# Chunk-selected attention and a gated MLP on one core: halved maxima for four pairs, not three, an order held as ranks, and the first tile's bounds left out

## The chip, the cores and the metric

The kernel runs on one core of a Trainium2 chip. A core has five engines that run their own instruction queues in order: TensorE (PE; its weight loads are listed as PEld), VectorE (DVE), ScalarE (ACT), GpSimd (POOL) and SyncE (SP, which here only issues DMAs). They wait for each other by semaphores. The metric is the device time of one execution in microseconds (us); a kernel's time is the median of its runs.

## The reference

Inputs are q, k and v of shape (4 batches, 8 heads, 768 tokens, 64), and the weights of a gated MLP. Attention reads only 6 chosen chunks of 32 keys per query; its output feeds the MLP:

```python
k_min, k_max = np.min(k_chunks, axis=3), np.max(k_chunks, axis=3)      # 24 chunks of 32 keys
ub = np.sum(np.maximum(q * k_min, q * k_max), axis=-1)                 # bound of a chunk's scores
ub = np.where(causal, ub, -1000000000.0)
top_chunks = np.argsort(ub, axis=-1)[..., -6:]
scores = scale * np.matmul(q, k.transpose(0, 1, 3, 2))
scores = np.where(sel & (pos[:, None] >= pos[None, :]), scores, -1000000000.0)
attn = np.exp(scores - np.max(scores, axis=-1, keepdims=True))
attn = attn / (np.sum(attn, axis=-1, keepdims=True) + 1e-09)
x = np.matmul(attn, v)                                                 # heads side by side: (4, 768, 512)
h = np.maximum(x @ w_in, 0.0); u, v = h[..., :512], h[..., 512:]
v_n = (v - mean(v)) / np.sqrt(var(v) + 1e-06)
out = (u * (np.einsum('ts,bsd->btd', w_spatial, v_n) + b_spatial[None, :, None])) @ w_out
```

## The kernel before

The work is cut into 16 *pairs* p of heads (4 per batch; the two heads lie on partitions 0 to 63 and 64 to 127) and into one gated MLP per batch b. Tokens go by 6 tiles i of 128. All of it is a list of 1,395 *pieces* (`work_list`, L251), each with a name, an engine or two that can do it, the pieces that it comes after, and the buffers that it fills and reads. For a pair they are, in this order:

- `load`, `cast` (L626, L635): k, q and v by DMA, mostly from SP, then as 16-bit numbers; `turn`/`kT`/`qT` bring k and q to head dimension by token, on TensorE with a copy on ScalarE or, for pairs 5 to 15, by a transposing DMA; `qp` (L679) is max(-q, 0).
- `ext` (L666, VectorE): maximum and negated minimum of each chunk of keys. `bounds` (L692, TensorE): the bound of each chunk for each query by three products per tile and head; for pairs below `EARLY` = 6 a product of `big` and `far` ahead of them pushes the future chunks down, for later pairs `ub` (L704) adds a constant. `top` and `leave` (L713, L720, VectorE): the sixth largest bound of tiles 1 to 5 and the chunks under it; tile 0 has but four chunks and none is left out.
- `pk` (L770, TensorE) and `mx` (L792, VectorE): all scores once, and each chunk's largest. For pairs below `FOLD` = 3 the part off the diagonal goes another way: `kd` (L738, GpSimd) is the difference of a chunk's two halves, `fd` (L742, TensorE) its product with q, `fr` (L751, ScalarE) the positive part, `fi` and `fb` (L755, L760, TensorE) add that to the scores of the second half, so that VectorE reads half as many numbers. The diagonal blocks (`end_product`, L730) are made alike for all.
- `minus`, `kept`, `shift`: the largest score over the chosen chunks (the shift of the exponential); `turn_bias` (L826, TensorE) and `bT` bring bias and shift to the other side, with six products of 64 rows, two at a time.
- `probs` (L843, TensorE): scores by key and query, with the bias added by a second product; `ex` (L867, ScalarE): the exponentials, in five strips of 512 columns and one of 128 for both heads; `cut` (L874, GpSimd): the causal part of the diagonal blocks; `weigh` (L880, TensorE): the product with v and a column of ones; `av`, `sum`, `inv`, `norm`: division by the sum, on GpSimd or VectorE; `xT`: transposed, mostly by a DMA from SP.

For a batch: `hv`, `vr`, `bn`, `rstd0` to `2`, `vn` (the normalised half), `hu`, `uT` (the other half), `mix`, `ms`, `plus`, `gT` (the spatial product, bias and gate), `og`, `oe`, `od` (the output). TensorE's PSUM has three buffers "two" for scores and exponents and two "mg" for the rest; in the last batch the MLP uses both.

What sets the order: `Work.order` (L114) runs a small planner, with a cost in us written beside each piece (`took` by engine) and a rank for each from the table `RANK`; each engine takes the ready piece of lowest rank whose buffers are free by the planner's clock. `WHERE` names the engine of each piece that has a choice. The result is one list, and each engine's instructions are issued in its order. Products of 64 rows (`TILED`, L100) and of 128 alternate in TensorE's queue.

Of the kernel before, what the change touches and what calls it, by code (L numbers as in the profile page):

```python
# [16 lines left out]
P = 128  # L17
# [66 lines left out]
"""  # L84
WHERE = """
AAAAGAGAGVGVGAAVAGAGAGVVAGAGAGAVVVVVAVAVAAAAAVVAVGGGGVGGAAVAAAAAAAAAAAVVAVAVVAAVAAVVGGGGGVVAAAAA
# [3 lines left out]
class Work:  # L90
# [8 lines left out]
    DELAY = {"PE": 0.25, "DVE": 0.17, "ACT": 0.18, "POOL": 0.14, "SP": 0.0}  # L99
    TILED = ("pk", "probs", "bounds", "turn_bias", "fd", "fb")  # L100
# [12 lines left out]

    def order(self):  # L114

        pieces, n = self.pieces, len(self.pieces)
        users, slot, freed_at, done_at = {}, {}, {}, {}
        slots = {tag: [None] * k for tag, k in self.bufs.items()}
        then, todo, ready_at, begun = [[] for _ in range(n)], [0] * n, [0.0] * n, [False] * n
        for i, (_, _, _, after, new, old, _) in enumerate(pieces):  # L120
            for b in new + old:
                users[b] = users.get(b, 0) + 1
            for a in after:
                then[self.index[a]].append(i)
                todo[i] += 1
        rank, where = [int(x) for x in RANK.split()], iter(WHERE.replace("\n", ""))
        engine = dict(P="PE", V="DVE", A="ACT", G="POOL", S="SP")
        assert len(rank) == n
        for i, (name, on, _, after, new, old, dma) in enumerate(pieces):
            if len(on) > 1:  # L130
                e = engine[next(where)]
                on = {e: on[e]}
# [934 lines left out]
```

## Time and profile before

| | |
|---|---|
| median of 3 runs | 249.05 us (248.89 to 249.26) |
| the profiled execution | 248.22 us, its span 246.5 us |
| PE busy | 224.9 us, 91% |
| DVE busy | 206.5 us, 84% |
| ACT busy | 191.9 us, 78% |
| POOL busy | 165.9 us, 67% |
| granted TensorE clock | 1.00 |

The span runs from the first instruction of an engine to the end of the last store. A line of a view by stage gives the busy time of each engine in a stretch; a line of the groups gives a source line, engine, operation, what it writes and reads, how often, its busy time and mean length, and the idle time before it with what ended it; a line of the chain gives a start, a length and what the end waited for.

### The profile page before, as it was taken

How to read it: one execution, taken by the hardware profiler on the slowest of the kernel's cores; microseconds unless marked ns; L12 is line 12 of the kernel's file. 1: busy time of each engine (PE TensorE's matmuls, PEld its weight loads, DVE VectorE, ACT ScalarE, POOL GpSimd, SP SyncE). 2: the span in 40 equal slices, each digit the busy share in tenths (PEclk: the TensorE clock that was granted, in tenths of full speed). 3: DMA queues.
4: the chain of work that ended last, by engine and by line, in shares of the span. 5: the costliest groups of instructions: out<-in, count | busy, mean ns of one | idle time of the engine just before them, and what ended most of it. 6: DMA issues, size and time to landing. Idle time of an engine off the chain costs nothing.

```text
span 246.5 us, 9019 instructions
## 1 busy us (share of the span) xinstructions
PE 224.9 (91%) x3780; PEld 144.6 (59%) x3780; DVE 206.5 (84%) x512; ACT 191.9 (78%) x298; POOL 165.9 (67%) x209
## 2 busy tenths in 40 slices
PE   0898778878999999999999999999999999999993
PEld 0656457666755675666665576666745566645551
DVE  4799999999999999799998997899998853349670
ACT  3598887979998999587859897897679969767312
POOL 8879749887785377999965929999926147402160
PEclk9999999999999999999999999999999999999999
DMA  7969996699999949484899997128900010350005
GB/s 189 325 186 201 257 242 127 122 164 241 168 186 235 216 82 187 89 170 112 190 161 271 175 200 125 34 75 140 268 22 19 0 36 0 105 188 0 0 28 227
DMA packets 93895, 35.51 MB, mean 144 GB/s; under 512 B 86208, under 2 KB 90144, under 8 KB 93856
## 3 DMA queue, kind: packets, MB, share of 16 engines
q1 hardware_dynamic: 91568, 31.81, 61.9%
q0 software_dynamic: 2016, 2.75, 6.5%
q8 instruction: 29, 0.48, 0.8%
q10 hardware_dynamic: 272, 0.39, 0.5%
q14 instruction: 10, 0.08, 0.1%
HBM read 24.77 MB, written 6.29 MB: 126 GB/s over the span
## 4 chain that ended last, share of the span: by engine, by line
PE 48%; DVE 28%; ACT 14%; DMA 4%; issue 3%; POOL 2%; DVEq 0%; ACTq 0%
DVE cmax L807 11%; PE mg L1001 11%; ACT pr L871 8%; PE mg L1024 6%; PE mg L885 5%; PE two L856 4%; PE mg L937 3%; PE two L863 3%; DVE stats L954 3%; DVE ext L671 3%; PE two L786 3%; DVE top L715 2%; PE mg L990 2%; DMA k<-in_k_dram 2%; DVE cmax L801 2%
## 5 line engine op out<-in xcount | busy, mean ns | idle before, releaser
L871 ACT ACTIVATE pr<-two 128x1024 f16<-128x1024 f32 (+1 forms) x96 | 85.3, 934 | 5.4 <-PE two L863 4.8
L807 DVE TENSOR_REDUCE cmax<-two 128x24 f32<-128x768 f32 (+4 forms) x104 | 85.3, 843 | 3.5 <-PE two L735 2.0
L856 PE MATMUL two<-qT,kT 64*128 64x128 f16 (+3 forms) x384 | 40.5, 258 | 5.4 <-ACT bT L835 1.9
L863 PE MATMUL two<-bT,member 64*128 64x128 f16 (+1 forms) x512 | 39.7, 233 | 0.0
L877 POOL TENSOR_SCALAR_AFFINE_SELECT pr<-pr 128x768 f16<-128x768 f16 x32 | 27.9, 886 | 9.1 <-ACT pr L871 9.0
L1019 POOL TENSOR_TENSOR vr<-tmp,uT 128x384 f16<-128x384 f32 x27 | 24.5, 922 | 11.9 <-DVE tmp L1012 11.8
L671 DVE TENSOR_REDUCE ext<-kT 128x24 f16<-128x768 f16 x32 | 29.5, 936 | 1.9 <-ACT kT L617 1.7
L1001 PE MATMUL mg<-wsT,vn 128*128 128x384 f16 x168 | 30.2, 327 | 0.0
L856 PEld LDWEIGHTS <-kT 64*128 64x128 f16 x384 | 19.9, 94 | 17.2 <-issue 15.1
L863 PEld LDWEIGHTS <-member 64*128 64x128 f16 x512 | 25.7, 94 | 5.1
L885 PE MATMUL mg<-v,pr 128*128 128x65 f16 x672 | 25.9, 194 | 0.7 <-POOL pr L877 0.5
L786 PE MATMUL two<-kT,qT 64*128 64x384 f16 (+4 forms) x182 | 24.6, 280 | 1.4 <-ACT pr L871 0.5
L885 PEld LDWEIGHTS <-pr 128*128 128x128 f16 x672 | 23.1, 98 | 3.6 <-issue 1.0
L1001 PEld LDWEIGHTS <-vn 128*128 128x128 f16 x192 | 17.7, 98 | 12.2 <-issue 0.6
L990 PE MATMUL mg<-xT,w_in_sb 128*128 128x384 f16 x112 | 22.4, 328 | 0.0
L907 POOL TENSOR_TENSOR x<-av,rc 128x768 f16<-128x768 f32 x11 | 16.2, 1469 | 8.8 <-DVE rc L900 4.9
L732 PE MATMUL two<-kT,qT 64*128 64x128 f16 x192 | 19.6, 221 | 2.3 <-ACT qT L617 1.0
L1024 PE MATMUL mg<-w_out_sb,vr 128*128 128x512 f16 x84 | 20.8, 380 | 0.0
L937 PE MATMUL mg<-w_in_sb,xT 128*128 128x512 f16 x84 | 20.3, 380 | 0.4 <-DVE o L619 0.4
L889 ACT COPY av<-mg 128x390 f32<-128x390 f32 x32 | 15.6, 500 | 6.2 <-PE mg L885 6.0
L954 DVE BATCH_NORM_STATS2 stats<-vr 128x6 f32<-128x512 f32 x24 | 16.6, 692 | 4.0 <-ACT vr L942 2.9
L735 PE MATMUL two<-half_ahead,ident 64*128 64x64 f16 x192 | 19.8, 193 | 0.0
(113 smaller groups left out, 496.8 us busy)
## 6 DMA issues: line engine op xcount, KB each, us to landing
q<-in_q_dram SPq DMA_DIRECT2D x16, 384.0 KB, 6.4
v<-in_v_dram SPq DMA_DIRECT2D x16, 384.0 KB, 5.7
out_dram<-o SPq DMA_DIRECT2D x24, 256.0 KB, 2.1
k<-in_k_dram SPq DMA_DIRECT2D x15, 384.0 KB, 5.7
vr<-in_moe_w_spatial_dram POOLq DMA_DIRECT2D x6, 192.0 KB, 5.6
w_in_sb<-in_moe_w_in_dram POOLq DMA_DIRECT2D x4, 256.0 KB, 8.8
w_out_sb<-in_moe_w_out_dram POOLq DMA_DIRECT2D x4, 128.0 KB, 4.5
k<-in_k_dram ACTq DMA_DIRECT2D x1, 384.0 KB, 4.7
```

Source lines behind the costliest of these rows:

```text
L671: nc.vector.tensor_reduce(held["ext", p][:, m], src, axis=AX.X, op=Alu.min if m else Alu.max, negate=(m == 1))
L786: mm(t[:, h, o:o + before], lhsT=qT[rows[h], c], rhs=kT[rows[h], a * CH:a * CH + before], start=True, stop=True)
L807: nc.vector.tensor_reduce(tops(p)[:, i // 2, :, i % 2, a:z], held["two", (p, u)][:, :, o:o + n].rearrange("p h (c e) -> p h c e", e=CH), a ...
L856: mm(t[:, h, z:z + n * P], lhsT=kT[rows[h], keys], rhs=qT[rows[h], i * P:(i + n) * P], start=True, stop=False)
L863: mm(d, lhsT=member[rows[h], r, keys], rhs=bT[rows[h], m * P:(m + w_) * P].rearrange("c (m s) -> c m s", s=P), start=False, stop=(n == 1 o ...
L871: nc.scalar.activation(out=held["pr", p][:, :, c0:c0 + n], in_=held["two", (p, "e", c0)][:, :, 0:n], func=Act.Exp, scale=scale)
L877: nc.gpsimd.affine_select(out=d, in_=d, compare_op=Alu.is_ge, fill=0.0, base=0, channel_multiplier=-1, pattern=[[0, NT], [1, P]])
L885: mm(a[:, i, :], lhsT=pr[:, at[t, i]:at[t, i] + P], rhs=vp[:, h * NT + t, :], start=(t == 0), stop=(t == i))
L937: mm(t, lhsT=held["xT", b][:, ko, i * P:(i + 1) * P], rhs=w_in_sb[:, ko, DH:2 * DH], start=(ko == 0), stop=(ko == NDO - 1))
L990: mm(t, lhsT=w_in_sb[:, ko, db * P:(db + 1) * P], rhs=held["xT", b][:, ko, s * HS:(s + 1) * HS], start=(ko == 0), stop=(ko == NDO - 1))
L1001: mm(t, lhsT=held["vn", b][:, si, db * P:(db + 1) * P], rhs=wsT[:, si, s * HS:(s + 1) * HS], start=(si == 0), stop=(si == NT - 1))
L1024: mm(t, lhsT=held["vr", ("g", b)][:, ko, i * P:(i + 1) * P], rhs=w_out_sb[:, ko, :], start=(ko == 0), stop=(ko == KO - 1))
```

## The change

1. `FOLD` is 4: pair 3's maxima are halved as those of pairs 0 to 2.
2. `bounds` leaves out the three products of tile 0; what remains for tile 0 is the product of `big` and `far`, for all pairs.
3. A `turn_bias` with neighbours of 128 rows on both sides in TensorE's queue is made with products of 128 rows (the other head's rows meet zeros of the identity), one at a time. In the new order these are pairs 5, 6 and 9.
4. `RANK` is a new table and is now the order itself, a permutation of the 1,398 pieces; the planner with its clock is gone, and a buffer goes to the slot whose last user stands earliest. `WHERE` is new too: `norm` is on GpSimd for 14 pairs (before 11), `gT` on VectorE for 10 pieces (before 5), and some single pieces change engines, among them `qp` of pair 0 (from ScalarE to VectorE).
5. Some costs in the list are other numbers; with the planner gone nothing reads them.

```diff
 RANK = """
-0 9 100 7 13 10 5 1 28 103 118 168 128 124 256 303 296 313 298 327 425 450 446 421 430 435 398 407 417 422 403 411 388
+1 12 207 2 21 5 4 3 81 366 138 175 174 164 200 276 322 321 287 320 570 565 564 413 435 440 419 421 402 409 383 394 393
...
 WHERE = """
-AAAAGAGAGVGVGAAVAGAGAGVVAGAGAGAVVVVVAVAVAAAAAVVAVGGGVGGAAVAAAAAAAAAAAVVAVAVVAAVAAVVGGGGGVVAAAAA
+AAVAGVGAGAGVGAAVAGAGAGAVVGAGAGVGAGAGAAAVAAAAAVVVVGVVVGVVAAAAAAAVAAAAVVVVVAAAAVAAVAGGVVGGVVAAAAVA
...
+    EITHER = ("turn_bias",)
...
+        for (name, on, _, _, _, _, _), at in zip(pieces, rank):
+            result[at] = name, engine[next(where)] if len(on) > 1 else next(iter(on)), at
+        done = set()
+        for at, (name, _, _) in enumerate(result):
+            _, _, _, after, new, old, _ = pieces[self.index[name]]
+            for b in new:
+                tenants = held[b[0]]
+                free = [(-1 if x is None else last[x], k) for k, x in enumerate(tenants) if x is None or users[x] == 0]
+                slot[b] = min(free)[1]
+                tenants[slot[b]] = b
...
-FOLD = 3
+FOLD = 4
...
+    turned = [name for name, e, _ in order if e == "PE"]
+    whole = {name[1] for a, name, z in zip(turned, turned[1:], turned[2:])
+             if name[0] in Work.EITHER and not (a[0] in Work.TILED or z[0] in Work.TILED)}
...
-            each = [(big, far[:, i])] * (p < EARLY) + [(qT[:, c], x[:, 0]), (qp[:, c], x[:, 0]), (qp[:, c], x[:, 1])]
+            each = [(big, far[:, i])] * (p < EARLY or i == 0) + [(qT[:, c], x[:, 0]), (qp[:, c], x[:, 0]), (qp[:, c], x[:, 1])] * (i > 0)
...
-                r = slice(g * D, (g + 1) * D)
-                mm(t[:, g, m * D:(m + 1) * D], lhsT=bias[slot["bias", p]][r, 4 * m:4 * m + 4, :].rearrange("p g c -> p (g c)"), rhs=ident[r, r], start=True, stop=True)
+                r, c = slice(g * D, (g + 1) * D), slice(0, P)
+                if p in whole:
+                    r, c = c, r
+                mm(t[:, g, m * D:(m + 1) * D], lhsT=bias[slot["bias", p]][r, 4 * m:4 * m + 4, :].rearrange("p g c -> p (g c)"),
+                   rhs=ident[r, c] if p in whole else ident[r, r], start=True, stop=True)
```

More of the change, by code (lines that the diff above doesn't have):

```diff
@@ L1 @@
-import heapq
 import math
@@ L116, in order @@
         pieces, n = self.pieces, len(self.pieces)
[L117 to L120, printed above, removed]
+        rank, where = [int(x) for x in RANK.split()], iter(WHERE.replace("\n", ""))
+        engine = dict(P="PE", V="DVE", A="ACT", G="POOL", S="SP")
+        assert sorted(rank) == list(range(n))
@@ L121, in order @@
+        users, slot, last, result = {}, {}, {}, [None] * n
+        held = {tag: [None] * k for tag, k in self.bufs.items()}
+        for _, _, _, _, new, old, _ in pieces:
             for b in new + old:
                 users[b] = users.get(b, 0) + 1
[L123 to L132, printed above, removed]
-            pieces[i] = (name, on, rank[i], after, new, old, dma)
-        free = {e: 0.0 for e in self.ENGINES}
-        ready = {e: [] for e in self.ENGINES}
-        events = [(0.0, i) for i in range(n) if todo[i] == 0]
-        t, bus, late, tiled, result = 0.0, 0.0, 0.0, False, []
-        def place(i):
-            got = []
-            if any(b not in slot for b in pieces[i][5]):
-                return None
-            for tag, key in pieces[i][4]:
-                for k, b in enumerate(slots[tag]):
-                    if b is None or freed_at.get(b, t + 1) <= t + 1e-9:
-                        got.append(((tag, key), k))
-                        break
-                else:
-                    return None
-            return got
@@ L153, in begin @@
-        def begin(e):
-            nonlocal bus, late, tiled
-            aside, found = [], False
-            while ready[e] and not found:
-                due, i = heapq.heappop(ready[e])
-                if begun[i]:
-                    continue
-                got = place(i)
-                if got is None:
-                    aside.append((due, i))
-                    continue
-                found = begun[i] = True
-                name, on, _, _, new, old, dma = pieces[i]
-                result.append((name, e, t))
-                took = on[e]
-                if e == "PE" and tiled != (name[0] in self.TILED):
-                    tiled, took = not tiled, took + 0.095
-                free[e] = t + took
-                if dma:
-                    if e == "POOL":
-                        late = max(late, t + took + 0.2)
-                        both = max(0.0, bus - late)
-                        bus += min(both, dma)
-                        late += 4 * dma if dma <= 0.25 * both else 0.75 * both + dma
-                        done = late + 0.8
-                    else:
-                        bus = max(bus, t + took + 0.4)
-                        both = max(0.0, late - bus)
-                        bus += 4 * dma if dma <= 0.25 * both else 0.75 * both + dma
-                        done = bus + 0.8
-                else:
-                    done = t + took + self.DELAY[e]
-                for b, k in got:
-                    slot[b] = k
-                    slots[b[0]][k] = b
-                for b in new + old:
-                    done_at[b] = max(done_at.get(b, 0.0), done)
-                    users[b] -= 1
-                    if users[b] == 0:
-                        freed_at[b] = done_at[b]
-                        heapq.heappush(events, (freed_at[b], -1))
-                for j in then[i]:
-                    todo[j] -= 1
-                    ready_at[j] = max(ready_at[j], done)
-                    if todo[j] == 0:
-                        heapq.heappush(events, (ready_at[j], j))
-            for x in aside:
-                heapq.heappush(ready[e], x)
-            return found
@@ L203, in order @@
-        heapq.heapify(events)
-        while len(result) < n:
-            while events and events[0][0] <= t + 1e-9:
-                i = heapq.heappop(events)[1]
-                if i >= 0:
-                    for e in pieces[i][1]:
-                        heapq.heappush(ready[e], (pieces[i][2], i))
-            while any([free[e] <= t + 1e-9 and begin(e) for e in self.ENGINES]):
-                pass
-            later = [f for f in free.values() if f > t + 1e-9] + [e[0] for e in events[:1]]
-            assert later or len(result) == n, "nothing can go on"
-            t = max(t, min(later, default=t))
+        for (name, on, _, _, _, _, _), at in zip(pieces, rank):
+            result[at] = name, engine[next(where)] if len(on) > 1 else next(iter(on)), at
@@ new lines, in order @@
+        done = set()
+        for at, (name, _, _) in enumerate(result):
+            _, _, _, after, new, old, _ = pieces[self.index[name]]
+            assert all(a in done for a in after) and all(b in slot for b in old), name
+            for b in new:
+                tenants = held[b[0]]
+                free = [(-1 if x is None else last[x], k) for k, x in enumerate(tenants) if x is None or users[x] == 0]
+                assert free, name
+                slot[b] = min(free)[1]
+                tenants[slot[b]] = b
+            for b in new + old:
+                users[b] -= 1
+                last[b] = at
+            done.add(name)
@@ L318, in work_list @@
         far_pe = p < EARLY
-        add("bounds", {"PE": (6 * far_pe + 18) * 0.027},
+        add("bounds", {"PE": 0.54 if far_pe else 0.412},
             DUE["bounds"],
@@ L396, in work_list @@
                 add("inv", {"DVE": 0.14}, at, 0, after=[("sum", p, 0)], old=[("rc", (p, 0))])
-                add("norm", {"POOL": 1.6, "DVE": 1.45}, at, 0, after=[("inv", p, 0)], old=[("av", p), ("rc", (p, 0))], new=[("x", p)])
+                add("norm", {"POOL": 1.5, "DVE": 1.15}, at, 0, after=[("inv", p, 0)], old=[("av", p), ("rc", (p, 0))], new=[("x", p)])
                 continue
@@ L431, in work_list @@
             group(i, "hv", NDO * col(DH), (i,), need + ([("og", b - 1, j) for j in range(NT)] if b else [("turn_ws", j) for j in range(NT)]), [("xT", b)], None, "vr", {"ACT": act(DH), "DVE": dve(DH)} if last else {"ACT": act(DH)}, "vr", i == 0)
-            add("bn", {"DVE": 0.87}, i, i, after=[("vr", b, i)], old=[("vr", b)])
+            add("bn", {"DVE": 0.89}, i, i, after=[("vr", b, i)], old=[("vr", b)])
         for g, rows in enumerate(TOGETHER[last]):
             add("rstd0", {"DVE": 0.08}, rows[-1] + 1, g, after=[("bn", b, i) for i in rows])
-            add("rstd1", {"POOL": 1.35}, rows[-1] + 1, g, after=[("rstd0", b, g)])
+            add("rstd1", {"POOL": 1.42}, rows[-1] + 1, g, after=[("rstd0", b, g)])
             add("rstd2", {"DVE": 0.1}, rows[-1] + 1, g, after=[("rstd1", b, g)])
@@ L449, in work_list @@
                 add("ms", {"ACT": act(HS)}, NT + 8 + m, db, s, after=[("mix", b, db, s)], old=[buf], new=[("tmp", (b, db, s))])
-                add("plus", {"POOL": 1.0}, NT + 8 + m, db, s, after=[("ms", b, db, s), ("b_load",)], old=[("tmp", (b, db, s))])
+                add("plus", {"POOL": 1.05}, NT + 8 + m, db, s, after=[("ms", b, db, s), ("b_load",)], old=[("tmp", (b, db, s))])
             else:
                 add("plus", {"DVE": 0.55}, NT + 8 + m, db, s, after=[("mix", b, db, s), ("b_load",)], old=[buf], new=[("tmp", (b, db, s))])
-            add("gT", {"POOL": 0.89, "DVE": 0.8} if b >= PLUS_POOL else {"POOL": 0.89}, NT + 8 + m, db, s, after=[("plus", b, db, s), ("uT", b, db, s)],
+            add("gT", {"POOL": 0.92, "DVE": 0.7} if b >= PLUS_POOL else {"POOL": 0.92}, NT + 8 + m, db, s, after=[("plus", b, db, s), ("uT", b, db, s)],
                 old=[("tmp", (b, db, s)), ("uT", b)] + ([("vr", ("g", b))] if m else []), new=[] if m else [("vr", ("g", b))])
```

1 line of the change is left out of this document (removed), and 100 rows, old and new, of the table RANK.

## The prediction

> **What bounds the kernel now.** I read the busy shares by stage first, then the chain that ended last, then the groups by line, and last the order of time at the start and at the last pair. The stages are cut where the first matmul starts (6.14 us), where VectorE stops being full (60), where the last pair is weighted (211), where the last batch's first product starts (219.15) and where the last matmul ends (242.80).
>
> ```profile
> 0.00:6.14 6.14, 0.00 (x1) 0.01 (x1) 3.02 (x20) 2.12 (x2) 4.95 (x18) 1.00 0.70 189
> 6.14:20.00 13.86, 12.14 (x261) 8.81 (x262) 11.79 (x26) 10.24 (x15) 11.31 (x15) 1.00 0.87 241
> 20.00:60.00 40.00, 32.77 (x828) 24.41 (x825) 39.19 (x109) 35.35 (x50) 31.29 (x45) 1.00 0.98 193
> 60.00:211.00 151.00, 149.21 (x2496) 94.98 (x2495) 133.32 (x318) 127.83 (x205) 109.12 (x125) 1.00 0.71 132
> 211.00:219.15 8.15, 7.20 (x73) 3.98 (x71) 3.42 (x7) 5.12 (x10) 2.49 (x2) 1.00 0.48 160
> 219.15:242.80 23.65, 23.59 (x128) 12.39 (x127) 15.71 (x34) 10.64 (x19) 6.71 (x7) 1.00 0.15 58
> 242.80:246.50 3.70, 0.00 (x0) 0.00 (x0) 0.00 (x0) 0.59 (x1) 0.00 (x0) 1.00 0.48 183
> ```
>
> Behind each stretch's length stand the busy times of PE, PEld, DVE, ACT and POOL, then the granted clock (1.00 throughout), the DMA share and GB/s. From 20 to 60 us VectorE is busy 39.19 of 40 us and TensorE 32.77: VectorE sets the pace. From 60 to 211 TensorE is busy 149.21 of 151, and from 219.15 it is busy 23.59 of 23.65; the last 3.70 are one copy and the store. So a microsecond of VectorE counts before 60 alone, and one of TensorE after 60.
>
> **The change, part by part: TensorE's own work.** Four edits touch it. The first is the number of changes between half-array products (64 rows, two at once) and whole-array ones. In the chain the same piece stands with a change beside it (158.49, 166.66) and, in the last batch, without one (236.59, 237.56):
>
> ```profile
> 158.49 1.08 PE mg L1001 x6
> ...
> 166.10 0.44 PE two L702 x36
> 166.66 0.97 PE mg L1024 x4
> ...
> 236.59 0.97 PE mg L1001 x6
> 237.56 0.86 PE mg L1024 x4
> ```
>
> A change costs 1.08 - 0.97 = 0.97 - 0.86 = 0.11 us. Counted in the two written orders, TensorE's queue goes from 172 changes to 158: 164 by the order, and six fewer because the turned biases of pairs 5, 6 and 9 now use the whole array between whole-array neighbours. Fourteen at 0.1 are -1.4 us; at least nothing, at most -1.5.
>
> The Trainium skill, "TensorEngine Tiling (Array Packing)", section "Tiling Modes", says that a change of tiling mode (not of tile) drains the engine, which agrees with the 0.11 above; it gives no price. "TensorE: Matmul & The Clock Gate", section "Single matmul latency", puts the array's drain at 128 cycles; at 2.4 GHz that is an estimate of 0.05 us, by which the fourteen would be worth -0.7. The measured 0.11 decides.
>
> Second, the bounds. Tile 0's three products for two heads go; pairs 0 to 5 keep its two "far" products, later pairs get two in exchange: 6 x 6 + 10 x 4 = 76 matmuls fewer. The row at 166.10 has 36 in 0.44 us, 12 ns each: -0.9. Third and fourth, pair 3's halving and the three whole-array bias turns, from the groups:
>
> ```profile
> L807 DVE TENSOR_REDUCE cmax<-two 128x24 f32<-128x768 f32 (+4 forms) x104 | 85.3, 843 | 3.5 <-PE two L735 2.0 <-PE two L786 1.3
> ...
> L786 PE MATMUL two<-kT,qT 64*128 64x384 f16 (+4 forms) x182 | 24.6, 280 | 1.4 <-ACT pr L871 0.5 <-DVE cmax L807 0.2
> ...
> L907 POOL TENSOR_TENSOR x<-av,rc 128x768 f16<-128x768 f32 x11 | 16.2, 1469 | 8.8 <-DVE rc L900 4.9 <-ACT bT L835 3.3 <-ACT pr L871 0.3
> ...
> L801 DVE TENSOR_REDUCE cmax<-two 128x16 f32<-128x256 f32 (+4 forms) x15 | 7.5, 542 | 0.2 <-PE two L766 0.2
> ...
> L753 ACT ACTIVATE fr<-two 128x896 f16<-128x896 f32 (+1 forms) x6 | 5.7, 972 | 0.9 <-PE two L748 0.9
> L795 DVE TENSOR_REDUCE cmax<-two 128x24 f32<-128x768 f32 x6 | 5.5, 946 | 0.0
> L907 DVE TENSOR_TENSOR x<-av,rc 128x768 f16<-128x768 f32 x5 | 5.0, 996 | 0.1
> ...
> L831 PE MATMUL two<-ident,bias 64*128 64x64 f16 x96 | 4.2, 192 | 0.6 <-DVE ub L619 0.3 <-DVE cmax L807 0.2
> ...
> L758 PE MATMUL two<-fr,ident 128*128 128x448 f16 (+1 forms) x12 | 3.8, 416 | 0.1
> L740 POOL TENSOR_TENSOR kd<-kT 128x384 f16<-128x384 f16 x3 | 3.0, 1007 | 0.7 <-ACT kT L617 0.7
> L748 PE MATMUL two<-kd,qT 64*128 64x256 f16 (+4 forms) x30 | 2.5, 281 | 0.2
> L766 PE MATMUL two<-kT,qT 64*128 64x256 f16 (+4 forms) x30 | 2.3, 264 | 0.0
> L690 DVE TENSOR_SCALAR qp<-qT 128x768 f16<-128x768 f16 x3 | 1.3, 424 | 0.2 <-DMA qT<-q 0.2
> ```
>
> Busy us and mean ns of one stand behind the bar. Three pairs are halved, thirteen are not. Halving a pair adds (2.5 + 3.8 + 2.3)/3 = 2.9 us of matmul and takes away 24.6/13 = 1.9: +1.0 (the diagonal products are the same 36). A bias turn takes 4.2/16 = 0.26 for six products in pairs; one at a time they could take up to twice that, and the cheapest is no more: 3 x (0 to 0.26), taken as +0.3. TensorE's sum is -1.4 - 0.9 + 1.0 + 0.3 = **-1.0 us**, between +1 (if changes save nothing and the turns double) and -1.4.
>
> **VectorE before 60 us.** A full pair's maxima take 85.3/13 = 6.6 us, a halved pair's (7.5 + 5.5)/3 = 4.3: pair 3 saves 2.2 us, in the stage where VectorE has 0.81 us to spare. ScalarE gets 5.7/3 = 1.9 us more (35.35 of 40 us busy there) and GpSimd 3.0/3 = 1.0 (31.29 of 40); both have cover, and without it the price is those numbers. Against it, pair 0's negated-and-clipped q goes from ScalarE to VectorE: from 0.42 (L690, from SBUF) up to the 0.83 that ScalarE takes below; I take 0.6, as VectorE's cast of as many elements, 0.56 (below), is nearest. Net on VectorE: -1.6.
>
> **The start.** The order there is new:
>
> ```profile
> 5.52 0.56 DVE L619 CAST k<-k 128x768 f16<-128x768 f32 x1 [1.97 <-DMA k<-in_k_dram]
> ...
> 7.00 0.80 ACT L617 COPY kT<-mg 128x768 f16<-128x768 f16 x1 [1.06 <-PE mg L652]
> ...
> 8.38 0.83 ACT L688 ACTIVATE qp<-mg 128x768 f16<-128x768 f16 x1
> 8.44 0.82 POOL L621 CAST k<-k 128x768 f16<-128x768 f32 x1 [0.89 <-DMA k<-in_k_dram]
> ...
> 9.23 0.91 POOL L740 TENSOR_TENSOR kd<-kT 128x384 f16<-128x384 f16 x1
> ...
> 10.69 0.40 ACT L617 COPY ub<-two 128x288 f32<-128x288 f32 x1 [1.48 <-PE two L702]
> ...
> 17.99 0.94 DVE L671 TENSOR_REDUCE ext<-kT 128x24 f16<-128x768 f16 x1
> ```
>
> The instructions that make the row pattern of the tile "member", by stretch (PE, PEld, DVE, POOL):
>
> ```profile
> 3.80:7.60 3.80, 0.00 (x0) 0.00 (x0) 0.00 (x0) 3.49 (x4) 1.00 1.17 313
> ```
>
> These four on GpSimd, 3.5 us, now stand behind the cast of pair 1's q and pair 0's half-difference. That one needs kT at 7.80, so it runs to about 8.8, the four to 12.3, and the cast of pair 2's k starts there instead of at 8.44. TensorE turns pair 2's k ahead of pair 0's first half-maxima, so these wait till about 13.5. And ScalarE copies pair 0's bounds behind two halving copies (0.95 each) and pair 1's q, at about 12 instead of 10.69, with VectorE's thresholds directly behind it. VectorE meanwhile has the diagonal maxima; walked with these durations it is at pair 1's extremes at about 18.2 us against 18.0 before, having done some 0.6 us less. Charge: **+0.8**, from 0 (SP brings pair 1's q before pair 0's v now, so the loads are in time) to 2.5, if GpSimd's late casts reach pair 1 too. Of the early relief 1.6 - 0.8 = **-0.8** is left. Nothing else on SP's queue moves ahead of what is due there: its late v loads and stores end up behind transposes whose readers come tens of us later.
>
> **The end.** Before, the last pair's weighting stood behind GpSimd's two causal cuts:
>
> ```profile
> 211.52 2.49 POOL L877 TENSOR_SCALAR_AFFINE_SELECT pr<-pr 128x768 f16<-128x768 f16 x2 [2.65 <-ACT pr L871]
> ...
> 214.06 0.84 PE L885 MATMUL mg<-v,pr 128*128 128x65 f16 x21 [0.50 <-POOL pr L877]
> ```
>
> Now the two exponentials that the cuts need are the first two of pair 15's on ScalarE's queue, where one of them was the last, and the cuts are off the path: up to the 0.95 that TensorE idles there (7.20 of 8.15). But the normalising of pairs 13 to 15 goes to GpSimd (1.47 against 1.00, two in a row at the end), with turn, copy and the last batch behind it and one output product fewer as cover: +0.5. Net **-0.4**, from -0.9 to +0.5. The last batch keeps its products; its vector work, spread anew, has 15.71 of 23.65 on VectorE before, so I cost that at nothing, and at up to +1 if one mix product waits.
>
> **ScalarE from 63 to 94.** Between the evictions of pair 3's and pair 5's second weighting the written order now puts four more wide exponentials and one narrow one on ScalarE (13 and 3 for 9 and 2), and four more exponent products and one more bounds piece on TensorE. That stretch was:
>
> ```profile
> 63.50:93.80 30.30, 29.83 (x514) 18.98 (x510) 29.34 (x69) 28.53 (x47) 19.04 (x24) 1.00 1.01 176
> ```
>
> and one run of exponentials, in order of time:
>
> ```profile
> 206.57 3.29 ACT L871 ACTIVATE pr<-two 128x256 f16<-128x256 f32 x4 [0.31 <-PE two L863]
> ```
>
> Three wide exponentials and a narrow one in a row take 3.29, so the five take some 4.2 and ScalarE needs 28.53 + 4.2 = 32.7. TensorE's products for a wide one stream 512 columns and 512 more for the mask in each half of the array; the row at 237.56 streams 2,048 in 0.86, so they take about 0.43. Four and a bounds piece (0.44) make 29.83 + 2.2 = 32.0. ScalarE goes past TensorE by 0.7 if it never idles, by 2.4 if it keeps its 1.77 idle. Its queue may run a little late without a wait for TensorE, since three PSUM buffers lie between: **+0.4**, from 0 to +2.4. Elsewhere from 60 to 211 the moves between VectorE, ScalarE and GpSimd lie beside TensorE's 149.21 of 151 and are costed at nothing; they could cost some tenths or win part of the 1.8 idle.
>
> **Sum.** -1.0 - 0.8 - 0.4 + 0.4 = -1.8 on the profiled execution: 248.22 us, of which 246.5 are the span and 1.7 lie around it, so 246.4. The median of the runs is 0.83 above it, 249.05, and against this I predict: 247.2.
>
> **The rivals.** *The relief passes whole*: the walk at the start is too dark, and VectorE's 2.2 us arrive undiminished: -2.2 - 1.0 - 0.4 = -3.6, with ScalarE never in the way: 245.5. For it: VectorE has no other spare time before 60. Against: the q edit added there. *GpSimd's casts hold the start*: these four ahead of pair 2's k also push the halving of pairs 1 and 2, and VectorE stands 2.5 us; of the early relief +0.9 is left, and -1.0 + 0.9 - 0.4 = -0.5 gives 248.6. It eats the whole relief once VectorE stands 1.6 us longer than now before 20 us. *ScalarE sets the pace from 63 to 94* (the slower side): TensorE waits the 2.4 us above, and since both meet at the end of that stretch, what VectorE won before it is not passed on, for ScalarE got 1.9 - 0.8 more there too, 36.4 against 35.35: -1.0 + 0 + 2.4 - 0.4 = +1.0, 250.0. It decides from the point where TensorE's waits on ScalarE there pass 1.4 us. For it: 28.53 of 30.30 before the addition; against: these are exponentials taken forward, whose place later in the queue falls free, and 0.7 is enough if none of them waits.
>
> The Trainium skill, "TensorEngine Tiling (Array Packing)", section "PSUM Bottleneck", says that tiling makes the products quicker and not the emptying of PSUM, so that this may bound next. The row 63.50 agrees that both emptying engines are near full (29.34 and 28.53 of 30.30).
>
> *That the change does not do what it says* can only concern the bias turns: three of sixteen qualify.
>
> **How the numbers follow.** Forecast 0.48 (247.2, its own range 246.0 to 248.4); relief whole 0.16; late start 0.13; ScalarE 0.23. A measurement of this kernel tells 0.2%, 0.5 us, from no change: 248.55 to 249.55 is the same, which takes most of the late start and the near edge of ScalarE. Faster 0.67, same 0.12, slower 0.21. The range 244.8 to 250.2 leaves about a tenth at either end.
>
> **What would show it.** Right: VectorE's maxima 2.2 us less before 60; TensorE's slices at nine or more from about 57 us; 76 fewer bounds products; no wait of the last weighting on GpSimd. Wrong: VectorE idle over 2 us between 8 and 20 us, TensorE's waits on ScalarE over 1.4 us between 63 and 94, or a new wait of a few tenths at many places from 60 to 211, where the new order was not walked piece by piece.

## The result, and the profile after

The changed kernel takes 252.66 us (median of 4 runs, 252.21 to 253.41) against 249.16 for the kernel before beside it (248.89 to 249.43): **1.0143 of the time before, 95% interval 1.0111 to 1.0176**. The prediction was 247.2, faster; the kernel is slower, and its time lies above the upper end of the predicted range (250.2). The profiled execution took 252.23 us, its span is 250.5.

The changed kernel by stage, with a stage of its own for the stretch where it idles and a new one behind the last pair's weighting (columns as in the prediction: PE, PEld, DVE, ACT and POOL busy, granted clock, DMA share, GB/s):

```profile
20.00:60.00 40.00, 32.36 (x787) 23.96 (x786) 37.86 (x107) 34.92 (x48) 32.19 (x46) 1.00 0.92 170
60.00:70.00 10.00, 7.19 (x129) 6.12 (x129) 5.80 (x11) 4.83 (x9) 2.89 (x5) 0.66 0.88 183
70.00:211.00 141.00, 138.81 (x2303) 88.12 (x2300) 127.89 (x307) 121.70 (x196) 101.66 (x117) 1.00 0.73 132
211.00:221.00 10.00, 9.99 (x133) 6.42 (x132) 5.07 (x10) 7.86 (x13) 7.37 (x7) 1.00 0.40 59
221.00:246.80 25.80, 25.56 (x142) 13.28 (x139) 17.11 (x37) 11.27 (x20) 7.07 (x7) 1.00 0.27 97
```

One stretch differs from all the others: from 60 to 70 us no engine is near full and the clock is 0.66. The same stretch finer, and TensorE's order of time in it:

```profile
59.00:61.00 2.00, 0.26 (x5) 0.08 (x2) 2.00 (x3) 1.55 (x2) 2.00 (x4) 1.00 1.24 229
61.00:63.00 2.00, 0.19 (x6) 0.20 (x8) 0.11 (x1) 0.00 (x0) 0.63 (x1) 0.73 1.10 226
63.00:65.00 2.00, 2.00 (x34) 1.51 (x31) 1.19 (x4) 0.86 (x2) 0.34 (x1) 0.50 0.05 10
```

```profile
62.81 0.29 PE L661 MATMUL two<-kT,qT 64*128 64x128 f16 x2 [3.55 <-DMA qT<-q]
```

TensorE stands 3.55 us for `qT` of pair 6 (the first of its maxima products, `pk` of pair 6) and then runs at half clock (0.50 from 63 to 67 us); from 69 to 71 us the clock is 1.00 again. Where that lateness came from, in the chain of waits of the changed kernel (start, length, what):

```profile
43.13 6.03 DMA q<-in_q_dram
...
49.22 0.82 POOL q L550
...
53.09 0.82 POOL k L550
...
55.25 7.51 DMA qT<-q
```

Pair 6's q is loaded at 43.13, cast at 49.22, its k cast at 53.09. On SP's queue the transposition of k, which needs that cast, stands ahead of the one of q; so the latter is issued at 55.25, and it lands 7.51 us later. In the order of time of the kernel before, the same steps on SP (loads of pair 6's q and k, transpositions of its k and q) and on GpSimd (casts of its q and k):

```profile
32.31 1.66 SPq L633 DMA_DIRECT2D q<-in_q_dram  x1
34.06 3.06 SPq L633 DMA_DIRECT2D k<-in_k_dram  x1
...
48.13 1.22 SPq L645 DMA_TRANSPOSE kT<-k  x1
49.44 1.24 SPq L645 DMA_TRANSPOSE qT<-q  x1
...
42.69 0.82 POOL L621 CAST q<-q 128x768 f16<-128x768 f32 x1
...
45.30 0.82 POOL L621 CAST k<-k 128x768 f16<-128x768 f32 x1
```

There the transposition of q is issued 5.8 us sooner, and it took 4.0 us. In the changed kernel both queues are reordered at this place. SP's queue has the transpositions of pair 5 ahead of pair 6's loads; the first waits until 40.35 us for a buffer that pair 1's last exponent product frees. And GpSimd's has pair 6's casts among pair 2's cuts, pair 5's v and blocks of the spatial weights:

```profile
40.35 1.41 SPq L574 DMA_TRANSPOSE qT<-q  x1
41.86 1.22 SPq L574 DMA_TRANSPOSE kT<-k  x1
43.13 0.58 SPq L562 DMA_DIRECT2D q<-in_q_dram  x1
...
44.51 3.76 SPq L562 DMA_DIRECT2D k<-in_k_dram  x1
...
53.95 1.21 SPq L574 DMA_TRANSPOSE kT<-k  x1
55.25 1.25 SPq L574 DMA_TRANSPOSE qT<-q  x1
...
54.63 1.68 POOL L531 DMA_DIRECT2D vr<-in_moe_w_spatial_dram  x3
```

### The profile page after: what moved, and what is told of

It is laid out like the page before. It is cut to its first block, busy times and chain, and to the rows that moved or that the text cites. A ratio compares the mean times of both kernels' runs of the same rounds, so it can differ in the third digit from the quotient of the medians.

```text
span 250.5 us, 8849 instructions
## 1 busy us (share of the span) xinstructions
PE 225.2 (90%) x3714; PEld 146.2 (58%) x3714; DVE 208.5 (83%) x514; ACT 193.4 (77%) x299; POOL 166.1 (66%) x208
## 4 chain that ended last, share of the span: by engine, by line
PE 50%; DVE 15%; ACT 11%; POOL 11%; DMA 9%; issue 3%; SPq 0%; POOLq 0%; ACTq 0%; DVEq 0%
DVE cmax L736 7%; PE mg L869 7%; PE mg L933 7%; PE mg L956 5%; PE mg L817 5%; PE mg L922 5%; PE two L788 4%; PE two L795 3%; DMA qT<-q 3%; ACT pr L803 3%; DMA q<-in_q_dram 2%; PE two L715 2%; POOL pr L809 2%; DVE bias L653 2%; DMA k<-in_k_dram 2%
## 5 line engine op out<-in xcount | busy, mean ns | idle before, releaser
L736 DVE TENSOR_REDUCE cmax<-two 128x24 f32<-128x768 f32 (+4 forms) x96 | 79.0, 845 | 8.3 <-PE two L664 6.9
L817 PE MATMUL mg<-v,pr 128*128 128x65 f16 x672 | 27.0, 197 | 0.3 <-POOL pr L809 0.3
L839 POOL TENSOR_TENSOR x<-av,rc 128x768 f16<-128x768 f32 x14 | 20.7, 1480 | 9.9 <-DVE rc L832 9.6
L951 POOL TENSOR_TENSOR vr<-tmp,uT 128x384 f16<-128x384 f32 x22 | 20.9, 966 | 9.4 <-DVE tmp L944 5.7
L817 PEld LDWEIGHTS <-pr 128*128 128x128 f16 x672 | 24.2, 100 | 3.8 <-POOL pr L809 0.7
L715 PE MATMUL two<-kT,qT 64*128 64x256 f16 (+4 forms) x168 | 23.8, 286 | 1.4 <-DVE cmax L736 0.7
L664 PE MATMUL two<-half_ahead,swap 64*128 64x64 f16 x192 | 19.1, 195 | 0.0
```

What stands on the lines that cost most here:

```text
L664: mm(t[:, h, d + m * D:d + (m + 1) * D], lhsT=(ident if m == h else swap)[h_rows[h]], rhs=half_ahead[h_rows[h]], start=False, stop=(m == 1))
L736: nc.vector.tensor_reduce(tops(p)[:, i // 2, :, i % 2, a:z], held["two", (p, u)][:, :, o:o + n].rearrange("p h (c e) -> p h c e", e=CH), a ...
L817: mm(a[:, i, :], lhsT=pr[:, at[t, i]:at[t, i] + P], rhs=vp[:, h * NT + t, :], start=(t == 0), stop=(t == i))
```

## The experiments

All ratios are to the kernel before, run beside it on the same chip, with 95% intervals; where two experiments are compared by their ratios, both intervals count. Edits of the order are shown on a stretch of an engine's queue, with ... for the pieces around it. A small helper that moves pieces in the list puts most lines of the experiments 32 further down than in the changed kernel (transpositions L606, casts L582). Where two profiles are compared by the start of "the same instruction", it is the same place in TensorE's queue, counted from each profile's first product (which comes 6.11 us into the changed kernel's profile and 5.66 into that of experiment 5).

**1. Pair 6's loads alone moved ahead on SP.** The first theory was SP's order.

```diff
 SP:  ... load.4.v
+     load.6.q load.6.k
      qT.5 kT.5
-     load.6.q
      load.5.v
-     load.6.k
      load.7.q kT.6 qT.6 ...
```

> The changed kernel with one thing different: on SP's queue the loads of pair 6's q and k stand ahead of the transposition of pair 5's q, which waits for a buffer until 40.35 us, as they did in the kernel before; nothing else is moved. Theory (queue order): the 3.55 us in which TensorE waits for pair 6's transposed q at 59 us go, and with them the clock of 0.62 to 0.69 that follows (about 2.5 us more); what is left is the forecast's relief, so 246 to 247.5 us, the granted clock 1.00 throughout. Rival (the new order is dear elsewhere from 60 us on, for example at ScalarE, and the wait only took time that would have been lost anyway): 249 to 250.5 us. Rival (traffic: the transposition is slow because of what moves beside it, whenever it is issued): the wait shrinks by less than half, over 250 us.

Measured: 251.93 us, 1.0138 (1.0103 to 1.0173): no gain. In the order of time of this run on SP and on GpSimd:

```profile
53.65 1.98 SPq L606 DMA_TRANSPOSE kT<-k  x1
55.73 1.25 SPq L606 DMA_TRANSPOSE qT<-q  x1
...
49.34 0.82 POOL L582 CAST q<-q 128x768 f16<-128x768 f32 x1
...
52.80 0.82 POOL L582 CAST k<-k 128x768 f16<-128x768 f32 x1
```

The loads were early, yet the casts stand where they stood (49.34 and 52.80), so the transpositions do too; TensorE waited 4.3 us. The theory falls as it was put: SP's order alone is not the cause. The rival that lays the loss elsewhere is not confirmed either, since the wait stayed. The traffic rival's signs came (over 250 us, a wait that did not shrink; the transposition took 7.9 us), but as it was issued no earlier than before, this run does not test it.

**2. The kernel before with pair 6's loads as late as in the changed one.**

```diff
 SP:  ... load.4.v
-     load.6.q load.6.k
      kT.5 qT.5
+     load.6.q
      load.5.v
+     load.6.k load.7.q
      kT.6 qT.6 load.7.k
-     load.7.q
```

> The kernel before with only SP's queue as in the changed one at this place: pair 6's q is loaded behind the transpositions of pair 5's q and k, pair 6's k behind pair 5's v, pair 7's q directly behind that. Theory (queue order): TensorE waits 2 to 4 us for pair 6's transposed q at about 59 to 63 us and its clock falls behind it, so 252 to 256 us against 249.2. Rivals that lay the loss on the rest of the new order: 249 to 250 us.

Measured: 255.61 us, 1.0286 (1.0249 to 1.0323). The time came as the theory had it, but not by its wait. GpSimd and TensorE in the order of time:

```profile
47.87 0.82 POOL L653 CAST q<-q 128x768 f16<-128x768 f32 x1 [5.50 <-DMA q<-in_q_dram]
...
54.41 0.82 PE L954 MATMUL mg<-ident,x 128*128 128x128 f16 x6 [5.77 <-POOL x L939]
```

In the order of before the cast stands early on GpSimd, so GpSimd itself stands 5.50 us for the late load, and behind it a normalisation for which TensorE waits 5.77. Late loads are dear, then, where the casts are early; where the casts are late too, they are hidden behind them.

**3. TensorE's wait filled.** 14 products of 512 columns ahead of `pk` of pair 6.

```diff
 def k_pk(e, p, u):
     t = new("two", (p, u), [P, 2, 512], F32)
+    if (p, u) == (6, 0):
+        for n in range(14):
+            mm(t[:, n % 2, :], lhsT=ident, rhs=member[:, 0, 0:512], start=True, stop=True)
```

> The changed kernel with 14 extra products of 512 columns (about 3 us of TensorE) put ahead of pair 6's first maxima product, where TensorE waits 3.55 us for the transposed q; they write the tile that the real products then overwrite. Theory (the fall of the clock is made by the idle stretch): the wait stays, filled, the clock stays at 1.00, and the kernel is about 2.5 us faster than the changed one, 249.5 to 250.5. If the clock fell for another reason: no gain, or a loss of some tenths, 252.5 to 253.5.

Measured: 250.59 us, 1.0086 (1.0057 to 1.0115). TensorE in the order of time, and the stretch behind the wait:

```profile
59.62 3.18 PE L704 MATMUL two<-member,ident 128*128 128x512 f16 x14
64.17 0.23 PE L661 MATMUL two<-kT,qT 64*128 64x128 f16 x2 [1.36 <-DMA qT<-q]
```

```profile
65.00:67.00 2.00, 2.00 (x54) 1.59 (x52) 2.00 (x7) 1.95 (x4) 0.82 (x1) 1.00 0.51 96
```

The product starts even later than before (64.17 for 62.81), and the kernel is still faster by 1.0143 - 1.0086 = 0.57%, 1.4 us: the clock stays at 1.00. The gain is smaller than the 2.5 us expected because of that later start, not because the fall is cheap: in the profiles the products stand 1.4 us later at the end of the wait and 1.0 earlier from 69 us on, with TensorE busy throughout in both. So the half clock cost about 2.4 us.

**4. Loads left late, traffic taken away.** Pair 7's q behind the transposition of pair 6's q; three blocks of spatial weights some 5 us later.

```diff
 SP:   ... load.6.k
-      load.7.q
       kT.6 qT.6
+      load.7.q
 POOL: ... kept.4
-      weights.ws.5 weights.ws.3 weights.ws.2
       norm.1 norm.2 cut.3.0
+      weights.ws.5 weights.ws.3 weights.ws.2
```

> The changed kernel with pair 6's loads left late, and the traffic beside the transposition of pair 6's q taken away: pair 7's q is loaded behind that transposition instead of ahead of it, and the last three blocks of the spatial weights are loaded behind the first causal cut of pair 3, some 5 us later. If lateness alone is enough: the transposition still lands after 60 us, TensorE waits 2 us or more, 250.5 to 252.5. If lateness only matters because traffic then makes the transposition take 7.5 us instead of 2.9: it lands at about 58, TensorE does not wait, 246 to 248.

Measured: 251.39 us, 1.0105 (1.0068 to 1.0143). The time is the first case's, but its wait of 2 us or more did not come; nor did the second case's landing at 58 us. TensorE in the order of time:

```profile
60.42 0.23 PE L693 MATMUL two<-kT,qT 64*128 64x128 f16 x2 [1.32 <-DMA qT<-q]
...
64.00 0.83 PE L849 MATMUL mg<-v,pr 128*128 128x65 f16 x21 [0.84 <-POOL pr L841]
...
66.22 0.61 PE L570 MATMUL mg<-ident,vr 128*128 128x128 f16 x4 [1.27 <-DMA vr<-in_moe_w_spatial_dram]
```

Issued at 55.87, the transposition landed after 4.5 us, and the wait was 1.32 instead of 3.55. But now the weights come late for their own turning, 1.27, and with the 0.84 ahead of it TensorE's clock still fell (0.50 from 67 to 69). With less traffic beside it the transposition was shorter (4.5 us for 7.5), but issued this late it still landed too late.

**5. Loads and casts of pair 6 moved ahead.** The second theory: pair 6's whole way, load, cast and transposition, is late on two queues.

```diff
 SP:   as in 1
 POOL: ... kept.3 weights.ws.1
+      cast.6.q cast.6.k
       cut.2.0
-      cast.6.q
       cut.2.1 cast.5.v weights.ws.4 minus.4
-      cast.6.k
       kept.4 ...
```

> The changed kernel with pair 6's q and k brought forward on both queues that hold them: the loads ahead of the transposition of pair 5's q on SP (as in the run where these alone were moved, which left the transposition at 55.73 us), and the two casts on GpSimd ahead of the causal cut of pair 2, with which they stood behind other pairs' work until 49.3 and 52.8. What the transpositions then wait for is their buffer, which pair 2's last exponent product frees at about 51.2 us. Theory (pair 6's q and k stand too late on GpSimd's queue): pair 6's q is transposed from about 52.5 us and has landed before TensorE asks for it at 59.3; no wait, no fall of the clock; 0.985 to 0.995 of the kernel before, which is the forecast's relief. Rival (traffic alone decides, and the blocks of the spatial weights still move beside it): it takes 7 us or more to land, TensorE waits 1 us or more, over 1.00 of the kernel before.

Measured: 246.85 us against 248.6, **0.9913 (0.9882 to 0.9943)**: the theory's case. SP and GpSimd in the order of time, and two stages:

```profile
50.96 1.22 SPq L606 DMA_TRANSPOSE kT<-k  x1
52.28 1.38 SPq L606 DMA_TRANSPOSE qT<-q  x1
...
46.90 0.83 POOL L582 CAST q<-q 128x768 f16<-128x768 f32 x1
47.67 0.83 POOL L582 CAST k<-k 128x768 f16<-128x768 f32 x1
```

```profile
60.00:95.00 35.00, 33.62 (x648) 23.34 (x647) 33.40 (x84) 33.97 (x57) 22.65 (x29) 1.00 1.21 182
...
211.00:217.70 6.70, 6.48 (x71) 3.69 (x69) 1.74 (x4) 4.89 (x8) 2.79 (x2) 1.00 0.86 183
```

Both transpositions follow the freeing of their buffer directly, q's lands at 57.6 and nobody waits for it. Against the changed kernel's profile the same instruction starts 4.93 us earlier from 69 us to the end, and 0.74 later up to 55 us (the start, see 12): 5.7 us are won in between. This kernel (kernel 5 below) beats both.

**6. The weights loaded earlier as well.** Kernel 5, with `weights.ws` 4, 5, 3 and 2 directly behind `weights.ws.1` on GpSimd.

> The run with pair 6's loads and casts brought forward, and beside it the last four blocks of the spatial weights loaded directly behind the second one (about 46 us) instead of at 51.9 and 54.6, so that they move ahead of the transpositions and not beside them. Theory (lateness and traffic together made the wait): the transposition lands in about 3 to 4 us; no wait at 59 us; at most 0.3 us better than the run without this edit, since the wait was gone there already. Rival (traffic alone): better by 2 us or more.

Measured: 248.19 us, 0.9976 (0.9958 to 0.9993): worse than 5 by 0.6%, which neither case had. The view of the DMAs gives for the transpositions of pair 6's k and q (us from issue to landing):

```profile
kT<-k SPq DMA_TRANSPOSE x1, 7.5
...
qT<-q SPq DMA_TRANSPOSE x1, 7.1
```

In 5 these were 5.6 and 5.3. The weights, issued at 45.87 to 48.6, took 6.7 us to land and so were still moving when the transpositions came. TensorE did not wait for the transposition, but 1.33 us at 58.4 us for something that the profile does not name; what that was stays open.

**7. The kernel before with the small TensorE edits.** Tile 0's bounds left out, and whole-array bias turns for the five pairs that qualify in its order (the lines of the turns are those of the change).

```diff
-    each = [(big, far[:, i])] * (p < EARLY) + [(qT[:, c], x[:, 0]), ...]
+    each = [(big, far[:, i])] * (p < EARLY or i == 0) + [(qT[:, c], x[:, 0]), ...] * (i > 0)
```

> The kernel before, in its own order, with only the small edits to TensorE's work: tile 0's three bound products left out (two far products in exchange for pairs 6 to 15), and the turned biases that stand between whole-array products in that order (pairs 1, 6, 9, 13 and 14) on the whole array. By the prediction's terms, 76 matmuls at 12 ns (0.9 us) and ten changes at 0.11 (1.1) less, five times 0 to 0.26 us more; what lies before 60 us is hidden behind VectorE. So 0.5 to 1.5 us faster than the kernel before, 0.994 to 0.998 of it. If the bounds or the changes cost nothing where they stand: the same time.

Measured: 248.79 us, 1.0022 (0.9998 to 1.0045): no gain. The stretch from 211 to 220 us in this run, and in the kernel before:

```profile
211.00:220.00 9.00, 7.53 (x74) 4.11 (x73) 3.42 (x7) 5.19 (x10) 2.49 (x2) 1.00 0.71 166
```

```profile
211.00:220.00 9.00, 8.05 (x77) 4.37 (x75) 3.42 (x7) 5.51 (x10) 2.49 (x2) 1.00 0.50 169
```

TensorE's busy time fell by 1.8 us (224.9 to 223.1) and its idle time grew instead, 0.5 of it here. In front of the last pair's cuts TensorE stands 0.50 us in both; what is new is a wait of 0.52 at 217.95 for an output copy on ScalarE, which itself stood 0.96 for a store. Up to there nothing was won: the products of the two profiles stand within 0.1 us of each other at 211 us, and 0.6 apart at the end. So in that order the work left out was not what set the time, and the end was lost to a store that the prediction's terms do not have.

**8. The casts alone.** Kernel 5 without moving the loads.

> The changed kernel with only the two casts of pair 6 brought forward on GpSimd's queue (ahead of the causal cut of pair 2); their loads on SP stay behind the transposition of pair 5's q, so that they land at about 49 us (q) and 53 (k). With the run that moves the loads alone and the one that moves both, this tells whether both moves are needed. If the late load is a cause of its own: GpSimd stands in front of the cast of k until about 53 us, pair 2's cuts, its weighting and all behind them move back by some 5 us, and the kernel is slower than the changed one, 1.02 to 1.04 of the kernel before. If the place of the casts was all: 0.99 to 1.00.

Measured: 250.64 us, 1.0082 (1.0054 to 1.011). GpSimd and TensorE in the order of time, and the clock behind the wait:

```profile
52.82 0.83 POOL L582 CAST k<-k 128x768 f16<-128x768 f32 x1 [3.09 <-DMA k<-in_k_dram]
...
54.53 1.91 PE L849 MATMUL mg<-v,pr 128*128 128x65 f16 x42 [2.42 <-POOL pr L841]
```

```profile
57.00:59.00 2.00, 1.91 (x68) 1.67 (x66) 1.04 (x2) 1.43 (x3) 1.92 (x5) 0.50 0.90 112
```

As in 2, GpSimd stands for the load, and TensorE 2.42 us for pair 2's cuts. Neither case came: the kernel is slower than 5, so the late load is a cause of its own, but it is faster than the changed one and far from 1.02. The transposition of q, issued at 54.98, landed after 2.9 us: the weights are held up behind the casts, so what was issued earlier had landed (a DMA share of 0.08 from 53 to 55 us), and only one block of weights, at 56.00, was issued beside it. So both moves are needed:

| | loads late | loads ahead |
|---|---|---|
| **casts late** | 1.0143 (the change) | 1.0138 |
| **casts ahead** | 1.0082 | 0.9913 |

**9. Kernel 5 with pair 3's maxima in full.** The two halvings replaced by seven products and eight maxima at the same places.

```diff
-   kd.3  pk.3.0 pk.3.1  fd.3.* fr.3.* fi.3.* fb.3.*  mx.3.0 ... mx.3.6
+   pk.3.0 ... pk.3.6  mx.3.0 ... mx.3.7
```

> The run with pair 6's loads and casts brought forward (0.9913 of the kernel before), with pair 3's maxima computed in full again: its two halvings (difference, four helper products, two copies on ScalarE) are replaced by seven full maxima products and their eight maxima on VectorE at the same places of the order. By the prediction's terms: VectorE gets 2.2 us more before 60, where it sets the pace; TensorE 1.0 us less; ScalarE 1.9 and GpSimd 1.0 less. If VectorE's relief before 60 us is what the halving is worth: slower by 0.8 to 2 us than with it (0.995 to 1.000 of the kernel before). If instead ScalarE, which the halving loads, sets the pace right behind: no slower, or up to 1 us faster (0.987 to 0.992).

Measured: 249.57 us, 1.0043 (1.0023 to 1.0063), 1.3% above 5. By the ratios that is some 3.2 us, more than the 0.8 to 2 expected; the two profiled executions differ by 2.6. In the profiles the same instruction starts 0.8 us later at 37 us, 1.9 at 50, 2.05 from 75 us to 211, and 2.30 at the end. The relief of VectorE is real and passes on whole.

**10. Kernel 5 without whole-array turns.**

```diff
-    EITHER = ("turn_bias",)
+    EITHER = ()
```

> The same run with the turned biases of pairs 5, 6 and 9 on half the array again, as all are in the kernel before. From the run of the kernel before with five whole turns: a whole turn took 0.34 us where the halved one took 0.26, and the change beside it saved 0.1 on either side; so undoing three costs about 3 x (0.2 - 0.08) = 0.36 us: 0.991 to 0.994 of the kernel before. If the whole turn's six products one after the other cost as much as the changes: no difference.

Measured: 247.35 us, 0.9946 (0.9925 to 0.9967). The interval overlaps that of 5, so the times do not tell the two apart. In the profiles the distance between the two grows by 0.33 us from 22 us to the end, about the 0.36 expected.

**11. Kernel 5 with two exponentials done twice.** `ex` of pair 4, strips at 512 and 1024.

> The same run with two of pair 4's wide exponentials done twice on ScalarE, at about 66 and 74 us, 0.95 us each more; the second writes the same values again. If ScalarE sets the pace there (the prediction's last term, +0.4 with a range of 0 to 2.4): the kernel is slower by 1.3 to 1.9 us than without them, 0.997 to 1.000 of the kernel before. If TensorE sets it and ScalarE has slack: slower by less than 0.6 us, 0.990 to 0.994.

Measured: 249.35 us, 1.0028 (1.0013 to 1.0043), 1.15% above 5, more than either case had. From 65 to 70 us in 11 and in 5:

```profile
65.00:70.00 5.00, 3.69 (x89) 2.95 (x88) 3.98 (x8) 4.97 (x7) 2.03 (x2) 1.00 1.20 210
```

```profile
65.00:70.00 5.00, 4.52 (x98) 3.54 (x96) 4.96 (x12) 5.00 (x8) 2.81 (x3) 1.00 1.24 160
```

ScalarE is full in both, TensorE loses what ScalarE gets: in the profiles, which tell more here than the ratios, the same instruction starts 1.78 us later at 75 us and 1.90 at the end, for 1.9 added. Here ScalarE sets the pace; VectorE, at 4.96 of 5 us in experiment 5, is close to it.

**12. Kernel 5 with the start filled.** Ten products of 128 columns ahead of pair 2's first difference product.

> The run with pair 6's loads and casts brought forward, and beside it ten extra products of 128 columns (about 0.5 us of TensorE) at the start, ahead of pair 2's first difference product, where TensorE waits 0.6 us for pair 2's transposed q at about 16 us; the real products overwrite what they write. In the profile of the run without them TensorE is busy 1.74 of the 3 us from 15 to 18, its clock then falls to 0.54 from 18 to 21, and pair 2's maxima products stand 0.75 us later than in the changed kernel's profile, whose start kept the clock at 1.00; all five runs without them showed a mean clock below 1.00. If the thin stretch at 15 to 18 us lets the clock fall: with it filled the mean clock is 1.00 in most runs and the kernel 0.5 to 0.8 us faster, 0.987 to 0.990 of the kernel before. If the fall has another cause: the same mean clock and time, 0.990 to 0.994.

Measured: 247.02 us, 0.9943 (0.9915 to 0.9971): no faster than 5, the second case's time. The mean clock was 1.00 in 3 of 12 runs and 0.991 to 0.997 in the others, and the three were not the fastest. In the profile the clock stayed at 1.00 at the start and pair 2 stood 0.74 us earlier than in 5, but only 0.38 of that was left at 64 us and 0.43 at the end. What makes the clock fall at the start is not settled by this.

## Why the prediction was wrong, step by step

**The step that failed** is one sentence: "Nothing else on SP's queue moves ahead of what is due there". The transpositions of pair 5 moved ahead of pair 6's loads there, and on GpSimd, whose queue was walked only up to pair 2, pair 6's casts moved behind pair 2's cuts. The rivals held a late start, a busy ScalarE and small waits, but no late load with a transposition behind it. The two moves together are worth 1.0143 - 0.9913 = 2.3%, 5.7 us. In the profiles of the changed kernel and of experiment 5 these are 3.5 us for the wait itself, 1.8 behind it up to 69 us, where the changed kernel runs at half clock (that costs 2.4 by experiment 3, and experiment 5 has waits of its own there), and 0.4 between 55 and 58 us. With them undone the kernel is 1.75 us faster than the one before (246.85 against 248.6); the sum had said 1.8. That this is close is partly luck, since its terms erred both ways:

- *VectorE, pair 3's halving, -2.2:* held. Experiment 9 lost 2.05 us in the profile, all before 75 us.
- *TensorE's sum, -1.0:* wrongly composed. The +1.0 for pair 3's halving lies before 60 us, where VectorE has the pace, and by experiment 9 it hid there: undoing the halving lost about all of VectorE's 2.2. The whole turns with their six changes gave 0.33 (0.3 by the prediction's terms, six at 0.1 less the turns' 0.3). The bounds and changes of experiment 7 gave nothing in the old order; in the new one no run measured the bounds and the other eight changes by themselves.
- *The start, +0.8:* the walk had pair 1's extremes at 18.2 us. In the order of time of the changed kernel on VectorE:

```profile
10.39 0.95 DVE L619 TENSOR_SCALAR qp<-mg 128x768 f16<-128x768 f16 x1
...
18.57 0.94 DVE L600 TENSOR_REDUCE ext<-kT 128x24 f16<-128x768 f16 x1
```

  `qp` on VectorE took 0.95, not 0.6, and the extremes came 0.4 later. What the walk did not have is TensorE's thin stretch at 15 to 18 us and a clock that can fall behind it (last section).
- *The end, -0.4:* about -0.7. In 5 TensorE idles 0.22 of 6.70 us there and no longer waits for the cuts; before, it idled 0.95 of 8.15.
- *ScalarE from 63 to 94, +0.4:* the place was right, for experiment 11 shows that ScalarE sets the pace from 65 to 70 us. TensorE's idle time grew by 0.9 (1.38 of the 35 us from 60 to 95 in 5; before, by its row below, 0.50). But of its waits there the profile puts 0.5 down to ScalarE and 0.9 to VectorE's maxima, so how much of the 0.9 is ScalarE's is not told apart. That rival had its turning point at 1.4 and was not reached.

```profile
60.00:95.00 35.00, 34.50 (x612) 22.70 (x611) 33.91 (x88) 32.77 (x53) 22.31 (x28) 1.00 1.05 179
```

Of what was to be seen, "TensorE's waits on ScalarE" were watched for between 63 and 94 us, and the loss came at 59 to 69, but by a DMA.

## What to carry to other kernels

When an order is rewritten, follow each operand along its whole way (load, cast, transposition, product) over all queues and compare its landing with the moment its reader asks; one instruction that waits for a buffer holds up every load behind it on an in-order queue. A way that is late on two queues has to be mended on both: one move alone gave 0 or 0.6%, both together 2.3%. And count a wait of TensorE of some 2 us or more with the lower clock behind it.

## What the runs showed of the hardware that was not expected

- *A transposing DMA's time depends on what moves beside it.* For pair 6's q, from issue to landing: 2.9 us (experiment 8, issued at 54.98), 4.0 (before), 4.5 (experiment 4), 5.3 (5), 7.1 (6), 7.5 (the change, issued at 55.25), 7.9 (1) and 8.1 (3). Issued at nearly the same time, the runs with 2.9 and 7.5 differ in the blocks of spatial weights: in the change one was issued at 51.88 and three at 54.63, in experiment 8 these four at 56.00 and 57.87. Experiment 4, which moved three of them and a load of q away, got 4.5; how much each transfer counts is not told apart.
- *The clock fell after shorter gaps than 3 us.* It was 0.50 behind 3.55 us of idle (the change), 2.42 (experiment 8) and 0.84 and 1.27 about 1 us apart (experiment 4), and stayed at 1.00 behind a single 1.32 (experiment 4, at 60.42) and 1.36 (experiment 3). The Trainium skill, "TensorE: Matmul & The Clock Gate", section "Why this matters for your kernels", in the table's row on avoiding throughput drops, asks for no idle gaps above about 3 us; the first number agrees, the next two say that less can be enough.
- *The same thin stretch can pass either way.* At 15 to 18 us TensorE was busy 1.63 of 3 us in the changed kernel's profile and the clock stayed at 1.00; in that of experiment 5 it was busy 1.74 and the clock was 0.54 from 18 to 21 us, 0.75 us lost by 22.
